# Moving the left-hand tiles of a two-layer attention kernel by 32 bytes, loading its first keys in three groups, and splitting its first weights earlier

## The chip, the cores and the metric

The kernel runs on one core of one Trainium2 chip. The metric is the device time of one execution in microseconds, lower is better; the time of a kernel is the median of several executions. The engines are named as in the profile: PE (TensorE, matmul), PEld (TensorE's weight load), DVE (VectorE), ACT (ScalarE), POOL (GpSimd) and SP (SyncE, which here issues most DMAs). SBUF is the on-chip memory with 128 partitions, PSUM the memory that matmuls write.

## What is computed

Two layers, each an attention block followed by a block in which only 8 chosen tokens go through a feed-forward net. Everything is float32, with 2048 tokens of width 1024 and 32 heads of width 32:

```python
def _A_ref(x, wqkv, wo):
    qkv = (x @ wqkv).reshape(B, S, 3, H, Dh).transpose(2, 0, 3, 1, 4)
    q, k, v = qkv[0], qkv[1], qkv[2]
    p = softmax(einsum("bhqd,bhkd->bhqk", q, k) * Dh ** -0.5)
    o = einsum("bhqk,bhkd->bhqd", p, v)
    return o.transpose(0, 2, 1, 3).reshape(B, S, D) @ wo

def _B_ref(x, w_r, w_gate, w_up, w_down):
    r = x @ w_r
    idx = argsort(-r)[:, :8]
    ...
    y = (silu(x_sel @ w_gate) * (x_sel @ w_up)) @ w_down
    return x + scatter(y * sigmoid(r_sel))

x = A_x
x = x + _A_ref(_layernorm(x), A_wqkv, A_wo)
x = x + _B_ref(_layernorm(x), B_w_r, B_w_gate, B_w_up, B_w_down)
x = x + _A_ref(_layernorm(x), A_wqkv, A_wo)
x = x + _B_ref(_layernorm(x), B_w_r, B_w_gate, B_w_up, B_w_down)
```

## The kernel before

`layer(n, ...)` is called for n = 0 and n = 1; its order of instructions is written out by hand. Each call has three stages.

**Projection** (`L559` to `L770`). Tokens go in four chunks (c = 0 to 3) of 512. A tile of 128 tokens is loaded (`ln_load`), its statistics are made on DVE and POOL (`ln_stat`, `L137` and `L138` on POOL), it is normalised in place (`ln_norm`, `L599`), transposed on PE (`ln_tr`, `L612`) and kept as a high part `xh` (ACT, `L613`) and a remainder `xl` (DVE, `L617`). The weight matrix comes in twelve blocks `wb` of 1 MB for each chunk: `load_w` issues the DMA into one of two `wraw` tiles, `split_w` makes a high part `wh` (ACT, `L584`) and a remainder `wl` (POOL, `L585`). Blocks 0 to 3 give queries, 4 to 7 keys, 8 to 11 values. A product of two float32 matrices is three passes, wh·xh, wl·xh and wh·xl (`passes`, `L634`), with 128x128 stationary operands and 512 moving columns. A block is two steps of 24 matmuls, so 48 matmuls. For queries and keys the weights are stationary and `xh`, `xl` move; for values it is the other way about. Step k counts from 0 to 95; b = k % 24 and c = k // 24. Before the first step of a block, `split_w` of the next block and `load_w` of the one after it are put in the program. Queries and keys go through tiles `hi` and `lo` to DRAM (`qh`, `ql`, `kh`, `kl`), values through `vn` to `vd`.

The first keys that attention needs (head group 0) are loaded back from DRAM into `ks0` by `load_k`: 12 DMAs for the 1536 tokens of chunks 0 to 2 after step (2, 23), 12 more for the last 512 tokens after step (3, 3), as `KEYS_AT` says. After step (2, 20) come two DMAs of ones and the 12 DMAs of the first two query tiles (`load_q`). All these are issued by SP, in program order, with the weight loads and the stores; an instruction of SP that waits holds up all behind it. In the fourth chunk PE also makes the first maxima of the scores (`pre_group`, `L523`).

**Attention** (`L772` to `L908`). 32 units of 16 steps. A step has four matmuls for a later unit's row maxima (`L523`), eight for the scores (`L538`), the exponentials on ACT into a tile `P` (`L878`) and eight for P·v (`L804`). A unit ends with the copy of its output to SBUF (`o<-pv`, `L829`). A head group is four units; even groups read keys from `ks0`, odd groups from `ks1`. POOL adds up the `P` tiles (`L814`).

**Output** (`L913` to `L1032`). o·wo in three passes again (`L991`), residual, the second layer norm, the choice of 8 tokens and the feed-forward, whose steps for layer 0 are spread into the projection of layer 1.

**Where the tiles lie.** A tile has the same byte address in all partitions. Pools are stacks: most grow from the left end of SBUF, those with side "right" from the right end. All left-hand tiles come after the small constants of pool `cons`, so a constant's size moves all of them. In the program as built, left-hand data tiles start at multiples of 64 bytes (layer 0's `xh` at 47424, layer 1's `wh` at 51520), right-hand ones at 32 past a multiple of 64 (layer 0's `wh` at 163808). Layer 0 has `wraw`, `wh`, `wl` and `xt` on the right, `xh`, `xl`, the query tiles and the outputs on the left. Layer 1 has `wraw`, `wh`, `wl`, `xt`, `xh` and `xl` all on the left and the query tiles on the right. In both layers `ks0` and the feed-forward's first weights are on the right, `ks1`, `P`, `v`, `acc` and the operands of `L991` on the left.

At the start of layer 0 the order is: loads of three token tiles and of weight blocks 8 and 9, statistics and normalisation of tokens tiles 0 and 1, `ln_tr(0)`, `ln_tr(1)`, then `split_w(2)` of block 8 in two halves, then the first step.

Of the kernel before, what the change touches and what calls it, by code (L numbers as in the profile page):

```python
# [8 lines left out]
F32 = mybir.dt.float32  # L9
# [9 lines left out]
S, D, H, DH, F = 2048, 1024, 32, 32, 3584  # L19
# [20 lines left out]
SLOT_ROWS = (64, 33)  # L40
SUM_AT = 22

KEYS_AT = {(2, 23): slice(0, 3 * 512), (3, 3): slice(3 * 512, S)}


def unit_events(last):
# [11 lines left out]
def tile_kernel(ctx, tc, x, wqkv, wo, w_r, w_gate, w_up, w_down, out):  # L58
# [8 lines left out]
    cons = ctx.enter_context(tc.tile_pool(name="cons", bufs=1))  # L67
# [4 lines left out]
    def dma(out, in_):  # L72
        f = [a.bitcast(F32) if a.dtype == F32R else a for a in (out, in_)]
        sync.dma_start(f[0], f[1])

    def ps_st():
        return psum.tile([128, 512], F32, name="st", bufs=3)

    def ps_pre():
        return psum.tile([128, 1024], F32, name="pre", bufs=2)  # L80
# [11 lines left out]
    pool.memset(one_c, 1.0)  # L92
    mone = cons.tile([128, 1], F32, name="mone")
    pool.memset(mone, -1.0)
    ones32 = cons.tile([128, 32], F32, name="ones32")
    pool.memset(ones32, 1.0)
    ones_row = dram.tile([1, 8192], F32R, name="ones_row")
# [372 lines left out]
    def layer(n, src, dst, prev=None):  # L470
# [22 lines left out]
        def load_k(g, h, i, sl=slice(0, S)):  # L493
            r = 64 * (h % 2) + 32 * (i % 2)
            dma(KS[g % 2][r:r + 32, h // 2, i // 2, sl], (kl if i == 1 else kh)[g, 32 * h:32 * h + 32, sl])
# [65 lines left out]
        with ExitStack() as pst:  # L561
# [16 lines left out]
            def split_w(parts=1):  # L578
                wb, raw = RAW.pop(0)
                wh, wl = (pr_.tile([128, 2048], F32R, name=i) for i in ("wh", "wl"))  # L580
                W[wb] = [w.rearrange("p (a c) -> p a c", a=KD if wb < 8 else 4) for w in (wh, wl)]
                for i in range(parts):
                    sl = slice(2048 // parts * i, 2048 // parts * (i + 1))
                    act.copy(wh[:, sl], raw[:, sl])  # L584
                    pool.tensor_tensor(wl[:, sl], raw[:, sl], wh[:, sl].bitcast(F32), op=OP.subtract)  # L585
                    yield

            def ln_load(t):
                XT[t] = pr_.tile([128, D], F32, name="xt", bufs=3)
                dma(XT[t], src[t * 128:(t + 1) * 128, :])  # L590
# [3 lines left out]
            def ln_stat(t):  # L594
                LS[t] = ln_stats(XT[t])
# [5 lines left out]
            def ln_tr(t, wide=True):  # L601
                c, i = divmod(t, 4)
                if i == 0:
                    XC[c] = (pw.tile([128, KD, 512], F32R, name="xh"), pw.tile([128, KD, 512], F32R, name="xl"))
                xh, xl = XC[c]
                sl = slice(i * 128, (i + 1) * 128)
                ps = [(slice(0, KD), ps_pre())] if wide else [(slice(4 * j, 4 * j + 4), ps_st()) for j in range(2)]
                ps = [(asl, p.rearrange("p (a c) -> p a c", c=128)) for asl, p in ps]
                for asl, p in ps:
                    for j in range(asl.stop - asl.start):  # L610
                        a = asl.start + j
                        pe.transpose(p[:, j, :], XT[t][:, a * 128:(a + 1) * 128], ident)  # L612
                    act.copy(xh[:, asl, sl], p)  # L613

                def low():
                    for asl, p in ps:
                        dve.tensor_tensor(xl[:, asl, sl], p, xh[:, asl, sl].bitcast(F32), op=OP.subtract)  # L617
                return low
# [85 lines left out]
            if n:  # L704
                for _ in range(4):
                    prev.tick()
            lo = ln_tr(0)
            ln_load(3)
            ln_stat(2)
            lo()  # L710
            lo = ln_tr(1)
            ln_load(4)
            if not n:
                list(split_w(2))
            lo()
            ln_norm(2)
            ln_stat(3)
# [7 lines left out]
            for k, (c, wb, i) in enumerate(steps):  # L725
# [31 lines left out]
                if norm and at % 4 == 2:  # L757
                    ln_tr(t)()
                    if t + 3 < NT - n:
                        ln_load(t + 3)  # L760
                if (c, b) in KEYS_AT:
                    for j in range(3):
                        for h in range(4):
                            load_k(0, h, j, KEYS_AT[c, b])
                if (c, b) == (2, 20):
# [267 lines left out]

    x3 = dram.tile([S, D], F32, name="x3")
    layer(1, x3, out, layer(0, x, x3)).finish()


# [24 lines left out]
```

## Time and profile before

| what | value |
|---|---|
| three executions | 4647.03, 4654.71, 4658.94 us; median 4654.71 us |
| the profiled execution's own time | 4656.52 us |
| its span, first to last instruction | 4654.5 us |
| mean granted TensorE clock | 0.987 |
| projection, layer 0 / layer 1 | about 15 to 595 us / 2287 to 2900 us |
| attention, layer 0 / layer 1 | about 595 to 2049 us / 2900 to 4357 us |

The profile is of one execution. Its page gives the busy time of each engine, the span in 40 slices, the DMA queues, the chain of work that ended last, and groups of instructions with their busy time, mean length and idle time before them. The timeline lists instructions in order of time: start, length, engine, line, operation, output and inputs (for a matmul the moving operand first, then the stationary one), and in brackets how long the engine sat idle before it and what ended that. Two matmuls overlap in these records, since the end of each is modelled; the distance between their starts is what a matmul costs.

### The profile page before, as it was taken

Reading aid. Unit: us, or ns where it says so; the run is one execution under the profiler, and the core shown is the slowest. Engines: PE = TensorE matmul, PEld = TensorE weight load, DVE = VectorE, ACT = ScalarE, POOL = GpSimd, SP = SyncE. Lnnn points to the kernel's source line nnn. Section 1 sums busy time; section 2 is a strip of 40 time slices with the busy share of each in tenths; the row PEclk is TensorE's granted clock in tenths of the full one; section 3 lists DMA queues with packets and bytes.
Section 4 is the critical chain, followed back from the end, with each engine's and each line's share of the span. In section 5 each row is a group of like instructions: output and inputs, shape, how many; then the busy total and the mean of one; then the engine's idle time right before and its main releaser. Section 6 shows DMA issues by size and latency. Waiting matters only on the chain. (4 is left out here: it accounts for less than half of the span.)

```text
span 4654.5 us, 73388 instructions
## 1 busy us (share of the span) xinstructions
PE 4542.4 (98%) x29228; PEld 2697.7 (58%) x29228; DVE 3185.8 (68%) x4899; ACT 2428.1 (52%) x2562; POOL 3212.2 (69%) x1233
## 2 busy tenths in 40 slices
PE   8999999999999999999899999999999999999996
PEld 7887755545555555548577777555555555554572
DVE  2211578888888888876522215888888888887763
ACT  3222266767667676760122222776767667677400
POOL 4444378989889898944433442888889889898441
PEclk9999999999999999999899999999999999999997
DMA  5756476867777777749578674777767768676598
GB/s 184 201 179 196 141 165 145 180 149 161 170 153 168 156 168 158 181 118 262 180 247 288 218 208 128 162 168 155 172 148 171 160 150 180 147 168 159 149 257 309
DMA packets 326598, 833.26 MB, mean 179 GB/s; under 512 B 43008, under 2 KB 158720, under 8 KB 277088
## 3 DMA queue, kind: packets, MB, share of 16 engines
q1 hardware_dynamic: 272720, 476.91, 34.5%
q0 software_dynamic: 45024, 325.41, 34.5%
q10 hardware_dynamic: 8512, 26.26, 2.1%
q8 instruction: 229, 3.75, 0.3%
q14 instruction: 113, 0.93, 0.1%
HBM read 384.14 MB, written 119.24 MB: 108 GB/s over the span
## 5 line engine op out<-in xcount | busy, mean ns | idle before, releaser
L531 DVE TENSOR_REDUCE nm<-st 128x1 f32<-128x512 f32 x3916 | 2433.8, 684 | 373.4 <-PE st L523 367.4
L878 ACT ACTIVATE P<-pre 128x1024 f32<-128x1024 f32 x2048 | 1985.8, 1022 | 719.7 <-PE pre L538 521.9
L814 POOL TENSOR_TENSOR acc<-acc,P 128x2048 f32<-128x2048 f32 x434 | 2105.5, 4851 | 87.3 <-DMA P<-P 80.3
L538 PE MATMUL pre<-q,ks 64*128 64x512 f32 (+1 forms) x8192 | 1138.3, 395 | 4.2 <-ACT P L878 4.2
L804 PE MATMUL pv<-P,v 128*32 128x512 f32 x8192 | 1091.4, 605 | 4.5 <-DMA v<-vd 4.5
L523 PEld LDWEIGHTS st<-ks,q 64*128 64x128 f32 x3916 | 546.8, 184 | 907.5 <-DVE nm L531 764.2
L523 PE MATMUL st<-ks,q 64*128 64x512 f32 x3916 | 986.5, 471 | 0.4
L585 POOL TENSOR_TENSOR wl<-wraw,wh 128x2048 fp32r<-128x2048 f32 (+1 forms) x97 | 442.7, 4564 | 653.6 <-ACT wh L584 645.1
L538 PEld LDWEIGHTS pre<-q,ks 64*128 64x128 f32 (+1 forms) x8192 | 772.8, 187 | 186.6 <-ACT P L878 57.3
L817 POOL DMA_DIRECT2D P<-P x310 | 298.4, 963 | 257.5 <-PE st L523 185.0
L649 DVE TENSOR_TENSOR lo<-st,hi 128x512 fp32r<-128x512 f32 x128 | 88.5, 692 | 566.1 <-ACT hi L648 547.6
L634 PE MATMUL st<-xh,wh 128*128 128x512 f32 x1024 | 410.0, 400 | 0.0
L634 PE MATMUL st<-xh,wl 128*128 128x512 f32 x1024 | 402.0, 393 | 4.4 <-POOL wl L585 4.4
L634 PE MATMUL st<-xl,wh 128*128 128x512 f32 x1024 | 403.1, 394 | 0.0
L648 ACT CAST hi<-st 128x512 fp32r<-128x512 f32 x128 | 75.1, 586 | 538.7 <-PE st L634 533.6
L804 PEld LDWEIGHTS pv<-P,v 128*32 128x32 f32 x8192 | 162.3, 108 | 260.7 <-issue 252.5
L814 POOL TENSOR_TENSOR acc<-P 128x2048 f32<-128x2048 f32 x62 | 295.2, 4762 | 9.7 <-ACT P L878 5.2
L991 PE MATMUL pre<-woh,ohl 128*128 128x512 f32 x1024 | 245.5, 398 | 18.8 <-DVE pre L1019 13.2
L584 ACT CAST wh<-wraw 128x2048 fp32r<-128x2048 f32 (+1 forms) x97 | 183.2, 1891 | 148.2 <-PE pre L634 71.2
L991 PEld LDWEIGHTS pre<-woh,ohl 128*128 128x128 f32 x1024 | 195.3, 192 | 66.8 <-issue 17.2
L634 PEld LDWEIGHTS st<-xh,wh 128*128 128x128 f32 x1024 | 193.1, 189 | 56.4 <-issue 8.9
L634 PEld LDWEIGHTS st<-xh,wl 128*128 128x128 f32 x1024 | 193.3, 189 | 46.5 <-POOL wl L585 5.2
(249 smaller groups left out, 2961.7 us busy)
## 6 DMA issues: line engine op xcount, KB each, us to landing
P<-P POOLq DMA_DIRECT2D x310, 1024.0 KB, 8.9
wraw<-in_A_wqkv_dram SPq DMA_DIRECT2D x96, 1024.0 KB
q<-qh SPq DMA_DIRECT2D x256, 128.0 KB
ks<-kh SPq DMA_DIRECT2D x112, 256.0 KB
vd<-vn SPq DMA_DIRECT2D x32, 512.0 KB
qh<-hi SPq DMA_DIRECT2D x64, 256.0 KB
ql<-lo SPq DMA_DIRECT2D x64, 256.0 KB
kh<-hi SPq DMA_DIRECT2D x64, 256.0 KB
```

The costliest lines, as they stand in the source:

```text
L523: pe.matmul(ps[b], Q[u][rows, i, 0, qt * 128:(qt + 1) * 128], KS[(u // QC) % 2][rows, i, 0, j * 512:(j + 1) * 512], start=True, stop=True, ...
L531: dve.tensor_reduce(NM[u][:, j, 2 * i + b:2 * i + b + 1, qt], ps[b], axis=AX.X, op=OP.max, negate=True)
L538: pe.matmul(p[:, b * 512:(b + 1) * 512], KS[(u // QC) % 2][rows, i, slot, kt * 128:(kt + 1) * 128], Q[u][rows, i, slot, :], start=(slot == ...
L584: act.copy(wh[:, sl], raw[:, sl])
L585: pool.tensor_tensor(wl[:, sl], raw[:, sl], wh[:, sl].bitcast(F32), op=OP.subtract)
L634: pe.matmul(p, *pair(a, l, r), start=(a == 0 and k == 0), stop=(a == KD - 1 and k == 2))
L649: dve.tensor_tensor(lo, p, hi.bitcast(F32), op=OP.subtract)
L804: pe.matmul(PV[u][32 * h:32 * h + 32, :], V[g][:, kt, 32 * h:32 * h + 32], P[s][:, h, :], start=(kt == 0), stop=(kt == NT - 1), tile_posit ...
L814: (dve if on_dve else pool).tensor_tensor(o, a, P[u * NT + k].rearrange("p h c -> p (h c)"), op=OP.add)
L817: pool.dma_start(P[u * NT + a], P[u * NT + b], accum_op=OP.add)
L878: act.activation(P[s][:, 2 * i:2 * i + 2, :].rearrange("p h c -> p (h c)"), p, AF.Exp, scale=SCALE)
L991: pe.matmul(p[:, bl], l[:, a, :], r[a][:, bl], start=(k == 0 and a == 0), stop=(k == 2 and a == KD - 1))
```

## The change

Three edits. The keys of head group 0 for the first three chunks are loaded in three groups of 12 DMAs of 512 tokens each, after steps (2, 14), (2, 17) and (2, 20), in place of one group of 12 DMAs of 1536 tokens after step (2, 23). A constant tile of 32 bytes, which nothing reads or writes, is added to `cons`; each left-hand tile from `ones32` on moves by 32 bytes, right-hand tiles stay. And in layer 0 the first half of the split of the first weight block is put ahead of the first transposes, the second half right behind them, in place of both halves behind the second transposes.

```diff
-KEYS_AT = {(2, 23): slice(0, 3 * 512), (3, 3): slice(3 * 512, S)}
+KEYS_AT = {(2, 14 + 3 * i): slice(i * 512, i * 512 + 512) for i in range(3)}
+KEYS_AT[3, 3] = slice(3 * 512, S)
...
     pool.memset(mone, -1.0)
+    cons.tile([128, 8], F32, name="pad")
     ones32 = cons.tile([128, 32], F32, name="ones32")
...
+            first_w = split_w(2) if not n else iter(())
+            next(first_w, None)
             lo = ln_tr(0)
+            list(first_w)
             ln_load(3)
             ln_stat(2)
             lo()
             lo = ln_tr(1)
             ln_load(4)
-            if not n:
-                list(split_w(2))
             lo()
             ln_norm(2)
             ln_stat(3)
```

On the engines this moves: on ACT the two half copies `wh` (`L584`) from behind both `xh` copies to before the first and between the two; on POOL the two half subtractions `wl` (`L585`) ahead of the statistics of token tile 2; on SP the key loads as said. PE's and DVE's order stays the same.

## The prediction

> **What bounds the kernel now.** I read the page's totals first, then PE's groups, then what PE waited for.
>
> ```profile
> span 4654.5 us, 73388 instructions
> PE 4542.4 (98%) x29228; PEld 2697.7 (58%) x29228; DVE 3185.8 (68%) x4899; ACT 2428.1 (52%) x2562; POOL 3212.2 (69%) x1233
> ```
>
> ```profile
> L804 PE MATMUL pv<-P,v 128*32 128x512 f32 x8192 | 1091.4, 605 | 4.5 <-DMA v<-vd 4.5
> L634 PE MATMUL st<-xh,wh 128*128 128x512 f32 x1024 | 410.0, 400 | 0.0
> L991 PE MATMUL pre<-woh,ohl 128*128 128x512 f32 x1024 | 245.5, 398 | 18.8 <-DVE pre L1019 13.2 <-ACT ohl L944 4.7 <-DVE ohl L945 0.6
> ```
>
> ```profile
> PE st L634 <- POOL wl L585: 4.4, 2, 2.4
> ```
>
> PE is busy for 98% of the span: 4654.5 − 4542.4 leaves 112 us without it. So two things can move the time: a wait of PE that goes or comes, and the pace of the matmuls themselves. All waits of projection matmuls (`L634`) for `wl` inside the run sum to 4.4 us in two places. The pace is the larger matter, and it is not the same in the two layers. These are the first matmuls of consecutive blocks in layer 0 and layer 1, two blocks of queries or keys and two of values, each with 48 matmuls in between and no wait:
>
> ```profile
> 402.61 0.39 PE L634 MATMUL pre<-wh,xh 128*128 128x512 f32 x1
> ...
> 413.85 0.40 PE L634 MATMUL pre<-wh,xh 128*128 128x512 f32 x1
> ...
> 436.34 0.40 PE L634 MATMUL st<-xh,wh 128*128 128x512 f32 x1
> ...
> 447.54 0.40 PE L634 MATMUL st<-xh,wh 128*128 128x512 f32 x1
> ```
>
> ```profile
> 2711.59 0.39 PE L634 MATMUL pre<-wh,xh 128*128 128x512 f32 x1
> ...
> 2722.47 0.39 PE L634 MATMUL pre<-wh,xh 128*128 128x512 f32 x1
> ...
> 2744.23 0.39 PE L634 MATMUL st<-xh,wh 128*128 128x512 f32 x1
> ...
> 2755.11 0.39 PE L634 MATMUL st<-xh,wh 128*128 128x512 f32 x1
> ```
>
> A block of values takes 413.85 − 402.61 = 11.24 us in layer 0 and 2722.47 − 2711.59 = 10.88 us in layer 1; a block of queries 447.54 − 436.34 = 11.20 against 2755.11 − 2744.23 = 10.88. That is 0.234 and 0.233 us from start to start against 0.227, the same instructions on the same shapes, with nothing idle. What differs is where the operands lie. In layer 0 one operand (`xh`, `xl`) starts at a multiple of 64 bytes and the other (`wh`, `wl`) 32 bytes past one; in layer 1 both start at multiples of 64.
>
> **The 32 bytes.** After the change layer 0's `xh` lies at 47456 and its `wh` still at 163808: both are 32 past a multiple of 64, so the two operands stand in step again, as in layer 1, though both off 64. No row has two 128-row operands of this kind both at 32. The bounds: if only the step between the operands counts, layer 0 gains 0.36 us in 16 value blocks and 0.32 us in 32 query and key blocks, 5.8 + 10.2 = 16.0 us, and layer 1 keeps its pace. If the offset of 32 itself costs, layer 0 gains nothing and layer 1 loses as much as layer 0 could have gained. Attention has all four combinations, and so says which is nearer. These are the output copies that end a group of four units: even groups (`ks0`, right) and odd ones (`ks1`, left), first layer 0 with queries on the left, then layer 1 with queries on the right.
>
> ```profile
> 964.24 0.59 ACT L829 COPY o<-pv 128x512 f32<-128x512 f32 x1
> ...
> 1147.36 0.59 ACT L829 COPY o<-pv 128x512 f32<-128x512 f32 x1
> ...
> 1330.51 0.59 ACT L829 COPY o<-pv 128x512 f32<-128x512 f32 x1
> ...
> 3269.46 0.59 ACT L829 COPY o<-pv 128x512 f32<-128x512 f32 x1
> ...
> 3452.70 0.59 ACT L829 COPY o<-pv 128x512 f32<-128x512 f32 x1
> ...
> 3635.88 0.59 ACT L829 COPY o<-pv 128x512 f32<-128x512 f32 x1
> ```
>
> Layer 0: even 183.12 us (queries at 0, keys at 32), odd 183.15 (both at 0). Layer 1: even 183.24 (both at 32), odd 183.18 (queries 32, keys 0). The attention matmuls with two operands at 32 pay 0.09 us in 183, 0.05%, against those with both at 0; an offset that cost 3% by itself would show here as several us. But the mixed groups aren't slower either, so these 64-row pairs hide the effect that the 128-row matmuls show, and the evidence is one-sided. I take the first bound, slightly cut: one block starts at the slow clock, and the fourth chunk has other matmuls between. 15.5 us off.
>
> For the rest of attention the same rows give the price: `q`, `ks` all at 32 is the 183.24 case, 0.1 us a group, under 1 us in all. `P` and `v` (`L804`) are both on the left and move together; I take zero, with 1 to 3 us either way for the range. `L991` has both operands on the left and keeps its step: zero. The other engines read and write the moved tiles too. They are off the path: in layer 0's attention PE is busy for 1448.32 of 1454 us, whatever they do.
>
> ```profile
> 595.00:2049.00 1454.00, 1448.32 (x10850) 723.37 (x10846) 1257.73 (x2021) 1022.75 (x1084) 1274.90 (x403) 1.00 0.73 160
> ```
>
> The Trainium skill's page "SBUF — State Buffer", section "Who interferes with whom", speaks against this term: it gives TensorE two independent read ports, one for the moving operand and one for the weight load, and says that PE never waits on anyone. By that rule the place of one operand beside the other can't matter and this term is 0; the 3% between the layers is then left without a cause, and no run here has yet shown that it is the place. It is the third case below.
>
> **The keys.** PE's two waits for `wl` come from SP's queue. The rows of layer 0, by SP, ACT and PE, and the block's start and the next one's; then the same block of layer 1:
>
> ```profile
> 438.10 2.39 SPq L74 DMA_DIRECT2D ks<-kh  x4
> ...
> 445.36 0.39 SPq L74 DMA_DIRECT2D wraw<-in_A_wqkv_dram  x1
> ```
>
> ```profile
> 454.47 1.90 ACT L584 CAST wh<-wraw 128x2048 fp32r<-128x2048 f32 x1 [6.14 <-DMA wraw<-in_A_wqkv_dram]
> ```
>
> ```profile
> 458.74 0.40 PE L634 MATMUL st<-xh,wh 128*128 128x512 f32 x1
> 461.08 0.50 PE L634 MATMUL st<-xh,wl 128*128 128x512 f32 x1 [1.94 <-POOL wl L585]
> ...
> 473.70 0.39 PE L634 MATMUL st<-xh,wh 128*128 128x512 f32 x1
> ```
>
> ```profile
> 2765.99 0.39 PE L634 MATMUL st<-xh,wh 128*128 128x512 f32 x1
> ...
> 2781.19 0.39 PE L634 MATMUL st<-xh,wh 128*128 128x512 f32 x1
> ```
>
> The twelve key DMAs hold SP from 438.10 to 445.36 (7.26 us), their data goes ahead of the weights', and ACT gets the block 6.14 us late. The block then takes 473.70 − 458.74 = 14.96 us against 11.20, 3.76 more: the wait and the slower matmuls behind it. In layer 1 it is 2781.19 − 2765.99 = 15.20 against 10.88, 4.32 more. With the keys gone from there the weight load is issued some 7 us earlier, more than the lateness: 8.1 us off.
>
> The keys come back as 36 DMAs, at about 7.26 / 12 = 0.6 us each, in three places. Behind the first two groups wait one pair of key stores and the two weight loads of this row:
>
> ```profile
> 392.44 7.04 SPq L74 DMA_DIRECT2D wraw<-in_A_wqkv_dram  x2
> ```
>
> They are for the blocks that start at 413.85 and, 11.24 us on, at 425.1. The first has 21.4 us, of which `wh` and `wl` (1.9 and 4.6 us, rows below) take 6.5; some 7 us of SP's time still leaves 7 for the transfer. I put these two groups at nothing, covered by that lead; without it they would cost what a late block costs, some 4 us. The third group stands ahead of the ones, the query loads and this weight load:
>
> ```profile
> 425.20 0.39 SPq L74 DMA_DIRECT2D wraw<-in_A_wqkv_dram  x1
> ```
>
> ```profile
> 437.54 1.91 ACT L584 CAST wh<-wraw 128x2048 fp32r<-128x2048 f32 x1
> ```
>
> ```profile
> 439.54 4.62 POOL L585 TENSOR_TENSOR wl<-wraw,wh 128x2048 fp32r<-128x2048 f32 x1 [7.59 <-ACT wh L584]
> ```
>
> Issued 7.3 us later, at 432.5, it would have to land by 437.5 to cost nothing. `wl` now ends at 439.54 + 4.62 = 444.16; PE needs it for the second matmul of the block at 447.54, so 3.6 us of lateness are free. The bounds are 0 (the load had several us to spare, as ACT shows no wait for it) and the whole of 3.76 and 4.32 us again. A third of the old group (a third of the bytes) is in front, so I take 0.5 us in each layer: 1 us back, 7.1 off.
>
> **The first weights.**
>
> ```profile
> 11.92 1.29 DVE L133 BATCH_NORM_STATS2 bst<-xt 128x6 f32<-128x512 f32 x2 [0.56 <-DMA xt<-in_A_x_dram]
> ...
> 14.51 3.79 ACT L584 CAST wh<-wraw 128x1024 fp32r<-128x1024 f32 x3
> ...
> 18.05 0.80 PE L634 MATMUL pre<-wl,xh 128*128 128x512 f32 x1 [1.64 <-POOL wl L585]
> ...
> 21.51 4.61 POOL L585 TENSOR_TENSOR wl<-wraw,wh 128x2048 fp32r<-128x2048 f32 x1
> 21.58 5.09 DVE L599 TENSOR_SCALAR xt<-xt,mv,rs 128x1024 f32<-128x1024 f32 x1 [1.60 <-POOL rs L138]
> ...
> 26.72 1.03 PE L612 MATMUL st<-ident,xt 128*128 128x128 f32 x6 [0.59 <-DVE xt L599]
> ```
>
> Token tile 2 was issued behind block 8's weights on the same queue and is there by 11.92, so the weights are too. The first half can be copied before 12 us in place of 14.51, and PE's first matmuls stop waiting for `wh` and `wl`: up to 4 us earlier. But token tile 3 holds PE next. Its normalisation (21.58, 5.09 us) ends with POOL's 4.61 us subtraction that began 0.07 us before it; its statistics now come behind both half subtractions on POOL, so it moves forward by 1 to 1.5 us only, and the 26.72 row with it. If the DMA comes late, ACT holds back the first `xh` by up to 1 us. Between −4 and +1 I take −1.3, by that row.
>
> **The sum.** −15.5 − 7.1 − 1.3 = −23.9 us against the profiled execution, 4656.5 us (span 4654.5 and 2.0 around it): 4632.6. That execution is 1.8 us above the median of the three, 4654.7, so for the median 4631.
>
> **The rivals.**
> - *The offset of 32 itself is slow* (slower). From the first block of layer 0 on, every 128-row three-pass matmul with an operand at 32 takes 0.0067 us more: layer 0 stays, layer 1 loses 16.0, the 1536 matmuls of `L991` lose 10.2, the waits give back 8.4: +17.8, so 4672. With a second charge for the second operand it is 16 + 16 + 10 more, about 4715. For it: each slow block has an operand at 32, no fast one has. Against it: the 183.24 us groups.
> - *The 32 bytes do nothing* and the layers differ for another reason: −8.4, so 4646. Against it: the pace is constant over all of layer 0's blocks and changes with nothing else that I can name.
> - *The wait moves one block ahead*: the third key group makes block 37 of the projection as late as block 38 was. The keys give nothing, −15.5 − 1.3 and perhaps 1 us more lost: 4639. For it: SP's order; against it: the 3.6 us of slack.
>
> **How the numbers follow.** Forecast 0.64, offset slow 0.17, nothing from the 32 bytes 0.12, wait moved 0.07. A measurement of this kernel can't tell less than 0.3%, 14 us, from no change: faster means under 4641, slower over 4669. The forecast's own range is 4620 to 4641 (start and keys at their better bounds and attention's 3 us at the low end, no more than half the keys at the high end). Faster: 0.62 of it and half of the moved wait, 0.66. Same: the rest of these and the 0.12, 0.17. Slower: 0.17. The overall range leaves out the slow rival alone: 4616 to 4656, with some us for the spread of 4647 to 4659 shown by three runs.
>
> **What would show it.** Layer 0's blocks at 10.88 us with a matmul every 0.227 us, layer 1's unchanged, attention groups within 183.1 to 183.3: the 32 bytes as forecast. Layer 1's blocks at 11.2 us or `L991` slower: the first rival. No wait of `L634` for `wl` near the fourth chunk's third block: the keys; one at its second block: the moved wait. First `L634` matmul before 14 us with token tile 3's transposes near 25.4: the start. I am wrong if layer 0's pace stays at 0.233.

## The result and the profile after

The changed kernel takes 4643.6 us (median of 15 executions, 4639.5 to 4649.0) against 4652.9 us before (median of 15, 4647.0 to 4663.3) in the same comparison: a ratio of 0.9977 with a 95% interval of 0.9969 to 0.9984. That is 9 us, where some 24 were forecast. The profiled execution took 4647.36 us, with a span of 4645.5.

The page of the changed kernel opens with the span and the busy time of each engine. The projection's lines have moved down by two: its matmuls are now `L636`, the transposes `L614`, the split `L586` and `L587`, the normalisation `L601`. The output's have moved by three: its product is `L994`.

```profile
span 4645.5 us, 73445 instructions
PE 4535.0 (98%) x29228; PEld 2692.4 (58%) x29228; DVE 3181.2 (68%) x4899; ACT 2428.6 (52%) x2562; POOL 3211.9 (69%) x1233
```

PE is busy 7.4 us less (4542.4 before) with the same 29228 matmuls. The timeline of PE has the first matmuls of the same blocks of 48 as those shown of before: in layer 0 two blocks of values and four of queries and keys, then in layer 1 two and three.

```profile
399.24 0.40 PE L636 MATMUL pre<-wh,xh 128*128 128x512 f32 x1
...
410.44 0.40 PE L636 MATMUL pre<-wh,xh 128*128 128x512 f32 x1
...
432.83 0.40 PE L636 MATMUL st<-xh,wh 128*128 128x512 f32 x1
...
444.03 0.40 PE L636 MATMUL st<-xh,wh 128*128 128x512 f32 x1
...
455.23 0.40 PE L636 MATMUL st<-xh,wh 128*128 128x512 f32 x1
...
466.43 0.40 PE L636 MATMUL st<-xh,wh 128*128 128x512 f32 x1
...
2707.02 0.39 PE L636 MATMUL pre<-wh,xh 128*128 128x512 f32 x1
...
2717.90 0.39 PE L636 MATMUL pre<-wh,xh 128*128 128x512 f32 x1
...
2750.54 0.39 PE L636 MATMUL st<-xh,wh 128*128 128x512 f32 x1
...
2762.29 0.39 PE L636 MATMUL st<-xh,wh 128*128 128x512 f32 x1
...
2773.17 0.39 PE L636 MATMUL st<-xh,wh 128*128 128x512 f32 x1
```

- *Pace.* A block of values in layer 0 takes 410.44 − 399.24 = 11.20 us (11.24 before), a block of queries 444.03 − 432.83 = 11.20 (11.20 before). Layer 1 stays at 2717.90 − 2707.02 = 10.88. So layer 0's pace hardly moved, and layer 1, which now has both operands 32 past a multiple of 64, did not move at all.
- *Late blocks.* In layer 0 the block that waited takes 466.43 − 455.23 = 11.20 us instead of 14.96, in layer 1 2773.17 − 2762.29 = 10.88 instead of 15.20. The block ahead of it is new on the list in layer 1: 2762.29 − 2750.54 = 11.75, 0.87 more than its neighbours.

The list of PE's waits shows the late blocks, the start and the output product:

```profile
PE pre L994 <- DVE pre L1022: 15.2, 8, 5.4
...
PE st L614 <- DVE xt L601: 8.8, 3, 5.1
...
PE st L636 <- POOL wl L587: 0.6, 1, 0.6
```

The two waits of query and key blocks for `wl`, 4.4 us, are one of 0.6 now. The waits of the transposes for normalised tokens grew from 5.7 (two) to 8.8 (three): some 5.1 us of each sum is one wait in layer 1 that stayed, and in layer 0 the wait for token tile 3 grew from 0.59 to 3.49. `L994`, the output product, waits 15.2 us for DVE against 13.2, and all its waits grew from 18.8 to 21.6, though the change only moves its tiles, all by the same 32 bytes.

### The profile page after: what moved, and what is told of

It reads as the page before. It is cut to its first block, busy times and chain, and to the rows that moved or that the text cites. A ratio compares the mean times of both kernels' runs of the same rounds, so it can differ in the third digit from the quotient of the medians.

```text
span 4645.5 us, 73445 instructions
## 1 busy us (share of the span) xinstructions
PE 4535.0 (98%) x29228; PEld 2692.4 (58%) x29228; DVE 3181.2 (68%) x4899; ACT 2428.6 (52%) x2562; POOL 3211.9 (69%) x1233
## 5 line engine op out<-in xcount | busy, mean ns | idle before, releaser
L587 POOL TENSOR_TENSOR wl<-wraw,wh 128x2048 fp32r<-128x2048 f32 (+1 forms) x97 | 442.4, 4561 | 643.5 <-ACT wh L586 634.8
L636 PE MATMUL st<-xh,wh 128*128 128x512 f32 x1024 | 406.4, 397 | 0.0
L636 PE MATMUL st<-xh,wl 128*128 128x512 f32 x1024 | 401.4, 392 | 0.6 <-POOL wl L587 0.6
L636 PE MATMUL st<-xl,wh 128*128 128x512 f32 x1024 | 401.7, 392 | 0.0
L994 PE MATMUL pre<-woh,ohl 128*128 128x512 f32 x1024 | 247.6, 400 | 21.6 <-DVE pre L1022 15.2
L586 ACT CAST wh<-wraw 128x2048 fp32r<-128x2048 f32 (+1 forms) x97 | 183.7, 1894 | 145.9 <-PE pre L636 78.5
L994 PEld LDWEIGHTS pre<-woh,ohl 128*128 128x128 f32 x1024 | 196.9, 194 | 70.4 <-issue 19.9
L636 PEld LDWEIGHTS st<-xh,wh 128*128 128x128 f32 x1024 | 192.5, 188 | 56.4 <-issue 9.0
L636 PEld LDWEIGHTS st<-xl,wh 128*128 128x128 f32 x1024 | 192.4, 188 | 43.1
```

What stands on the lines that cost most here:

```text
L636: pe.matmul(p, *pair(a, l, r), start=(a == 0 and k == 0), stop=(a == KD - 1 and k == 2))
L994: pe.matmul(p[:, bl], l[:, a, :], r[a][:, bl], start=(k == 0 and a == 0), stop=(k == 2 and a == KD - 1))
```

## The experiments

The question after the result: why do layer 0's matmuls start every 233 ns and layer 1's every 227, if not by the offset modulo 64? Two theories, and a third that blames nothing in particular. *Step theory*: what counts is the distance between `xh` and `wh` modulo some larger power of two. *Side theory*: what counts is that one operand lies at the left end of SBUF and the other at the right. *Third theory*: something else of layer 0.

**Padding further, and moving the weights.** All three start from the changed kernel. The first two only change the size of the pad (40 numbers are 160 bytes; 168 in its place are 672), the third only the side of layer 0's weight pool.

```diff
-    cons.tile([128, 8], F32, name="pad")
+    cons.tile([128, 40], F32, name="pad")
```

```diff
-            pr_ = pst.enter_context(sbuf(f"pw{n}", bufs=2, side=None if prev else "right"))
+            pr_ = pst.enter_context(sbuf(f"pw{n}", bufs=2, side=None))
```

> The changed kernel with a pad of 160 bytes in place of 32: layer 0's xh at 47584, wh at 163808, a distance that is a multiple of 512 (but 512 past a multiple of 1024); after the change as given it was 128 past a multiple of 256. Step theory (the pace depends on the distance of the two operands modulo a power of two, 64 was too small): with 512 as the modulus, layer 0's blocks fall from 10.92 us first matmul to last to 10.65, as in layer 1, 48 x 0.27 = 13 us off, so about 4631 us. Side theory (what counts is that one operand lies at the left end of SBUF and the other at the right): blocks stay at 10.9 to 11.0 us and the time at 4642 to 4646. Third theory (something else of layer 0, not the place): the same as the side theory here.

> The changed kernel with a pad of 672 bytes: layer 0's xh at 48096, wh at 163808, a distance that is a multiple of 1024 (and not of 4096). Step theory with 512 or 1024 as the modulus: blocks of layer 0 at 10.65 us, about 4631 us; if the 160-byte pad stays slow and this one is fast, the modulus is 1024. Side theory and third theory: 10.9 to 11.0 us, 4642 to 4646.

> The changed kernel with layer 0's pool of wraw, xt, wh and wl on the left, where xh and xl lie (wh 76128, xh 108896; distance a multiple of 4096). Side theory: blocks of layer 0 at 10.65 us as in layer 1, 48 x 0.27 = 13 us off, 4629 to 4632. Step theory: the same, since the operands also come in step; the two are told apart by the padded kernels. Third theory (something else of layer 0): blocks stay at 10.9 us, 4642 to 4646.

In one comparison with the kernel before (4668.0 us): 160 bytes 4643.5 us, ratio 0.9957 (0.9940 to 0.9973); 672 bytes 4642.3, 0.9956 (0.9939 to 0.9972); weights on the left 4641.9, 0.9945 (0.9929 to 0.9962). The timeline of the 160-byte pad has layer 0's blocks of values, then of queries:

```profile
391.93 0.39 PE L636 MATMUL pre<-wh,xh 128*128 128x512 f32 x1
...
402.81 0.39 PE L636 MATMUL pre<-wh,xh 128*128 128x512 f32 x1
...
424.57 0.39 PE L636 MATMUL st<-xh,wh 128*128 128x512 f32 x1
...
435.45 0.39 PE L636 MATMUL st<-xh,wh 128*128 128x512 f32 x1
```

402.81 − 391.93 = 10.88 us, 435.45 − 424.57 = 10.88: layer 1's pace, in layer 0, with the operands still at opposite ends. The other two kernels have the same 10.88. So the side theory and the third theory fall, and the modulus is at most 512.

**Which modulus, and can layer 1 be made slow?** Two more pad sizes (104 numbers, 416 bytes, and 32 numbers, 128 bytes), and the weights on the left again with a gap of 128 bytes between the two pools in both layers:

```diff
-    cons.tile([128, 8], F32, name="pad")
+    cons.tile([128, 104], F32, name="pad")
```

```diff
+            pst.enter_context(sbuf(f"gap{n}")).tile([128, 32], F32, name="gap")
             pw = pst.enter_context(sbuf(f"pj{n}", bufs=2))
```

> The changed kernel with a pad of 416 bytes: the distance of layer 0's xh and wh is 256 past a multiple of 512. If the modulus is 256: blocks of layer 0 at 10.65 us as with 160. If it is 512: 10.9 us or more.

> The changed kernel with a pad of 128 bytes: the distance is 32 past a multiple of 512, where it was 160 past before the change (a matmul every 233.5 ns), 128 after it (232.4) and 0 with the pad of 160 (226.7). Step theory with any distance off the modulus slow: 232 to 234 ns, blocks at 10.9 to 11.0. If the cost grows with the distance: about 227 to 229 ns, 10.65 to 10.75.

> Layer 0's weights on the left beside xh as in the same-side run, but with a gap tile of 128 bytes between the two pools in both layers, so that the distance of xh from wh is 128 past a multiple of 512 in layer 0 and in layer 1 too. Step theory with 512 (or 256) as the modulus: blocks of both layers at 10.9 us first to last, a matmul every 232 ns, although all operands lie on one side; layer 1, which was at 10.65 in every run so far, becomes slow for the first time. Side theory: 10.65 us in both layers.

One execution each, beside 4666.5 us for the kernel before: 416 bytes 4637.4 us, 128 bytes 4663.2, the gap 4676.3; being single executions, they are read by their pace. Their totals hold more than that: from the last `o<-pv` copy of layer 0 to layer 1's first projection matmul the 128-byte pad took 284.7 us and the gap 283.3, against 272 to 279 in the other twelve profiles, and why stays open. Blocks of values with 416 bytes, blocks of queries with 128 bytes, and blocks of queries in layer 1 of the kernel with the gap:

```profile
392.15 0.39 PE L636 MATMUL pre<-wh,xh 128*128 128x512 f32 x1
...
403.03 0.39 PE L636 MATMUL pre<-wh,xh 128*128 128x512 f32 x1
```

```profile
436.75 0.40 PE L636 MATMUL st<-xh,wh 128*128 128x512 f32 x1
...
447.95 0.40 PE L636 MATMUL st<-xh,wh 128*128 128x512 f32 x1
```

```profile
2759.49 0.40 PE L636 MATMUL st<-xh,wh 128*128 128x512 f32 x1
...
2770.68 0.40 PE L636 MATMUL st<-xh,wh 128*128 128x512 f32 x1
```

10.88 us at a distance of 256, 11.20 at 32, and layer 1 is slow for the first time: 2770.68 − 2759.49 = 11.19, though all its operands lie at one end. Together, with the distance of `wh` from `xh` in the programs as built, and the spacing of matmuls (for each block the median distance of three starts, divided by three; mean over a layer's 48 blocks):

| kernel | layer 0: distance mod 256 | layer 0: ns | layer 1: distance mod 256 | layer 1: ns |
|---|---|---|---|---|
| before, keys alone | 160 | 233.7 | 0 | 227.0 to 227.1 |
| after, pad alone, late first weights | 128 | 232.6 to 232.8 | 0 | 227.0 to 227.1 |
| pad 128 | 32 | 233.3 | 0 | 226.7 |
| pad 160, 672, 416 | 0 | 227.0 | 0 | 226.9 to 227.0 |
| weights on the left | 0 | 226.9 | 0 | 227.1 |
| weights on the left, gap 128 | 128 | 233.4 | 128 | 233.0 |

Of the powers of two the modulus is 256: 128 is slow, and 256 past a multiple of 512 is fast. The place of the pair as a whole doesn't matter: in step, both operands lay 64, 96, 192 or 224 past a multiple of 256, and all of these ran at 227 ns. The cost is one of in step or out of it: 32 bytes off costs as much as 128 or 160, some 6 ns per matmul. Over 48 x 48 matmuls of a layer, 2304 x (232.8 − 227.0) ns = 13.4 us stayed unclaimed in the changed kernel. The three timed kernels in step lie 0.0020 to 0.0032 below the changed kernel's ratio of 0.9977, which is 9 to 15 us, each by an interval of some 8 us either way.

**Which pair must be in step?** The 160-byte pad with `wh` alone moved off by 128, in both layers:

```diff
-                wh, wl = (pr_.tile([128, 2048], F32R, name=i) for i in ("wh", "wl"))
+                wh = pr_.tile([128, 2048], F32R, name="wh")
+                if not W:
+                    pr_.tile([128, 32], F32, name="gap", bufs=1)
+                wl = pr_.tile([128, 2048], F32R, name="wl")
```

> The pad of 160 bytes, and a gap of 128 bytes between wh and wl, in both layers: now xh, xl and wl are in step modulo 256 and wh alone is 128 off them. In a block of queries or keys the matmuls go wh.xh, wl.xh, wh.xl with w stationary. If what counts is the weight load that runs beside a matmul (the next one's) against the data that this matmul streams: the intervals that begin with wl.xh and wh.xl are slow (next load wh), those that begin with wh.xh fast (next load wl). If what counts is a matmul's own two operands: those of wh.xh and wh.xl are slow, of wl.xh fast. In both cases two of three are slow, the mean is 230 to 231 ns, and blocks take 10.8 us in both layers.

A block of values, then one of queries, in layer 0:

```profile
401.23 0.39 PE L639 MATMUL pre<-wh,xh 128*128 128x512 f32 x1
...
412.22 0.39 PE L639 MATMUL pre<-wh,xh 128*128 128x512 f32 x1
...
434.19 0.39 PE L639 MATMUL st<-xh,wh 128*128 128x512 f32 x1
...
445.39 0.40 PE L639 MATMUL st<-xh,wh 128*128 128x512 f32 x1
```

The one execution took 4660.7 us, beside 4657.9 for the kernel before. Neither prediction came out. Queries and keys, with the weights stationary, are as slow as with everything out of step (445.39 − 434.19 = 11.20 us; intervals that begin with wh·xh, wl·xh, wh·xl of 233, 235 and 232 ns in the median of layer 0), so no interval is fast. Values, with the weights moving, lose a third of it (412.22 − 401.23 = 10.99; 233, 226 and 228 ns). Which reads meet, and why, stays open; the rule that holds over the other kernels is that all four tiles be in step.

**Each edit alone.** The keys in three groups alone, the pad of 32 bytes alone, and the change without the early first weights:

```diff
-KEYS_AT = {(2, 23): slice(0, 3 * 512), (3, 3): slice(3 * 512, S)}
+KEYS_AT = {(2, 14 + 3 * i): slice(i * 512, i * 512 + 512) for i in range(3)}
+KEYS_AT[3, 3] = slice(3 * 512, S)
```

> The kernel before with the keys in three groups as the only edit. My step by step account: the late block of layer 0 (14.73 us first to last) falls to 11.0 and that of layer 1 (14.97) to 10.65, less 0.9 us at the block after it in layer 1, as seen in the changed kernel: 7.2 us off, 4645 to 4646 (ratio 0.9985). Rival (the keys give nothing, since another block becomes late): 4652 to 4654, ratio 1.000.

```diff
     pool.memset(mone, -1.0)
+    cons.tile([128, 8], F32, name="pad")
```

> The kernel before with the pad of 32 bytes as the only edit. Modulus 256: the distance goes from 160 to 128 past a multiple of 256, still out of step; blocks of layer 0 fall from 11.0 us to 10.92, 48 times 0.05 to 0.08 us, so 2.5 to 4 us off; late blocks and start as before. Ratio 0.999 to 1.000, about 4 of the 9 us of the whole change at most. My forecast had given this edit 15.5 us: ratio 0.9967.

```diff
-            first_w = split_w(2) if not n else iter(())
-            next(first_w, None)
             lo = ln_tr(0)
-            list(first_w)
...
             ln_load(4)
+            if not n:
+                list(split_w(2))
```

> The changed kernel with the first weights split late, as before. In the changed kernel block 9 starts at 31.7 us instead of 33.4, but in the six other runs that split early it starts at 33.0 to 34.4 (best apart), because PE waits longer for token tile 3 and then runs at the slow clock. If early weights are worth nothing on the whole: block 9 at 33.2 to 33.6 here, and the time within 2 us of the changed kernel, ratio 0.998 of before. If they are worth the 1.3 us that I forecast, the same within what can be timed: the block's start decides, 33.3 against the mean of the early ones, 33.2.

Keys alone: ratio 0.9978 (0.9969 to 0.9988), in the comparison in which before was 4668.0 us, so 6 to 14 us off. Pad alone: 0.9990 (0.9980 to 0.9999); without early weights: 0.9974 (0.9965 to 0.9984), both beside a before of 4657.9 us. The once late blocks of the two layers with the keys alone:

```profile
458.67 0.40 PE L635 MATMUL st<-xh,wh 128*128 128x512 f32 x1
...
469.87 0.40 PE L635 MATMUL st<-xh,wh 128*128 128x512 f32 x1
...
2770.05 0.39 PE L635 MATMUL st<-xh,wh 128*128 128x512 f32 x1
...
2780.93 0.39 PE L635 MATMUL st<-xh,wh 128*128 128x512 f32 x1
```

11.20 and 10.88 us: nothing late is left, 3.76 + 4.32 = 8.1 us off. The block ahead of it is late in some runs and not in others: over the twelve kernels that carry the keys' edit, the changed kernel among them, it takes up to 0.6 us too long in layer 0 and up to 1.6 in layer 1.

The pad alone gives the pace of the changed kernel (232.7 ns) and no more. Its interval is 0.5 to 9 us off, and the pace accounts for 2304 x 1.0 ns = 2.3. The old late blocks are still there, that of layer 1 with 17.8 us in this profile, and its span of 4655.7 us is no shorter than before.

The early weights can't be told from nothing in the time. Block 9, the second block that layer 0 runs, starts at 33.4, 33.3, 33.0 and 32.6 us in the four kernels so far that split late (before, keys alone, pad alone, this one; mean 33.1) and at 31.7, 33.0, 34.2, 34.3, 34.0, 33.2, 34.4 and 34.1 in the eight that split early (mean 33.6). What takes the gain away stands in the start of the changed kernel and of the 672-byte pad. The changed kernel's timeline, and its windows (columns: stretch, length, then the busy time of PE, PEld, DVE, ACT and POOL, granted clock, DMA share, GB/s):

```profile
13.88 0.50 PE L636 MATMUL pre<-wh,xh 128*128 128x512 f32 x1 [0.76 <-DVE xl L619]
...
16.73 0.81 DVE L601 TENSOR_SCALAR xt<-xt,mv,rs 128x1024 f32<-128x1024 f32 x1 [1.11 <-POOL rs L140]
...
19.85 4.54 POOL L587 TENSOR_TENSOR wl<-wraw,wh 128x2048 fp32r<-128x2048 f32 x1
19.92 5.01 DVE L601 TENSOR_SCALAR xt<-xt,mv,rs 128x1024 f32<-128x1024 f32 x1 [0.94 <-POOL rs L140]
...
24.99 1.26 PE L614 MATMUL st<-ident,xt 128*128 128x128 f32 x8 [3.49 <-DVE xt L601]
```

```profile
25.00:28.00 3.00, 3.00 (x17) 2.46 (x18) 2.83 (x5) 1.18 (x2) 0.00 (x0) 1.00 0.22 72
```

The same in the kernel with the 672-byte pad:

```profile
25.20 1.97 PE L614 MATMUL st<-ident,xt 128*128 128x128 f32 x8 [3.52 <-DVE xt L601]
```

```profile
25.00:28.00 3.00, 2.80 (x11) 2.61 (x12) 2.21 (x5) 1.17 (x2) 0.00 (x0) 0.50 0.00 0
```

PE starts earlier, runs out of work earlier, and waits longer for token tile 3: 3.5 us in both. In one run it comes back at the full clock, in the other at 0.50, with transposes of 1.97 us in place of 1.26. Block 9 then starts at 34.2 in place of 31.7. Of the eight kernels that split early, the changed kernel's profile is the only one with the full clock from 25 to 28 us; the other seven have 0.50 there, five of them behind a pause of about 3.5 us, two (the 160- and the 416-byte pad) behind one of 2.64 and 2.74. The Trainium skill's page "TensorE: Matmul & The Clock Gate", section "Part 1: The HAM clock gate", has the clock decided over free-running windows of some 3.4 us. By that rule a pause of about that length would cool PE in one run and not in another, as in the two rows above; the pauses of 2.64 and 2.74 us are shorter than such a window, and it doesn't explain them by itself.

**A version faster than both.** The 160-byte pad, and the split of block 9 in four pieces, so that POOL's subtraction doesn't hold DVE for 4.5 us; with the first weights early, and with them late:

```diff
-                    list(split_w())
+                    list(split_w(1 if n or k else 4))
```

> The 160-byte pad, and block 9's split (copies wh and subtractions wl, at the first step of layer 0) in four parts instead of one. In all runs DVE's normalisation of token tile 3 takes 5.0 us beside POOL's 4.5 us subtraction and 0.8 us without it. If it only waits for POOL's instruction to end: it gets in after the first of four parts, 1.2 us, ends near 22 instead of 25, and the first block ends some 3 us earlier, near 30 us; the total is some 3 us below the 160-byte pad, 4627 to 4641 on its chip, ratio to before 0.995. If DVE is held back by POOL's work as such, whatever the size of the pieces: normalisation stays near 5 us, no gain over the 160-byte pad.

> The best version so far (160-byte pad, block 9's split in four parts) with the first weights split late as in the kernel before. If early weights help once token tile 3 no longer holds PE up: block 9 starts 1 to 1.5 us later than the 29.2 us with them, and the total is 1 us more. If they help nothing: 29.2 and the same total, ratio 0.9948.

With early weights: 4640.9 us, ratio 0.9948 (0.9934 to 0.9962), beside 4666.5 before. With late ones: 4630.2 us, 0.9940 (0.9926 to 0.9953), beside 4657.9 on another chip. The two intervals overlap; both lie clear of the change as given (0.9969 to 0.9984), though each was compared with the kernel before and never with the changed kernel directly. They also overlap that of the 160-byte pad alone (0.9940 to 0.9973), so what the four pieces add isn't shown in the time, only at the start. The start with early weights:

```profile
20.55 5.49 POOL L587 TENSOR_TENSOR wl<-wraw,wh 128x512 fp32r<-128x512 f32 x4
...
20.62 1.77 DVE L601 TENSOR_SCALAR xt<-xt,mv,rs 128x1024 f32<-128x1024 f32 x1 [0.94 <-POOL rs L140]
...
22.88 1.04 PE L614 MATMUL st<-ident,xt 128*128 128x128 f32 x8
...
29.24 0.39 PE L636 MATMUL pre<-wh,xh 128*128 128x512 f32 x1
```

DVE gets in behind the first piece: 1.77 us in place of 5.01, and the transposes wait for nothing. Block 9 starts at 29.2 us with early weights and at 32.3 with late ones, so in this version, by one profile of each, the early weights are worth 3 us at the start, more than the 1 to 1.5 expected. The total doesn't show it; the span from the last projection matmul of layer 1 to the end alone ranged from 1751 to 1761 us over the fourteen profiles.

## Why the prediction was right or wrong

- **What bounds the kernel** held: the time moved with PE's pace and PE's waits. The block behind the late one of layer 0 starts at 466.43 in place of 473.70, 7.3 us earlier: 1.7 from the start, 3.8 from the late block, and 38 of 48 blocks of the pace below, 1.7, make 7.2.
- **The 32 bytes: the failed step.** The step was "I take the first bound, slightly cut", that is, that "the two operands stand in step again" when both are 32 past a multiple of 64: 15.5 us. Both paces were read rightly, and that the place of one operand against the other makes the difference is now shown. But the step is modulo 256, not 64. The change took the distance from 160 to 128, out of step to out of step, and the pace from 233.7 to 232.8 ns: about 2304 x 0.9 ns = 2.1 us. The only two distances that the profile of before had were 160 and 0, so it could not tell a modulus of 64 from one of 256; with the addresses 47424 and 163808 at hand, the other powers of two that fit should have been bounds of their own.
- **The keys** came out as the sum said: 3.76 and 4.32 us off, 0 and 0.87 back (0.5 in each was taken), −7.2 against −7.1. The first two groups cost nothing, as put.
- **The first weights** gave −1.7 us in the profiled run (PE's first matmul 15.61 to 13.88, the transposes of tile 3 26.72 to 24.99, forecast near 25.4), −1.3 were forecast. That it came out near the forecast is luck: in the other seven early-split profiles PE came out of its pause at half the clock, and block 9 started at 33.0 to 34.4 us, against a mean of 33.1 with late splits. What was missed is that a pause of PE behind an earlier start can cost the clock.
- **The sum.** Measured in the two profiles: −2.1 − 7.2 − 1.7 = −11.0 us; the spans differ by 9.0. The 2 us between lie behind the projection: from the last `o<-pv` copy of layer 0 to layer 1's first projection matmul it took 275.7 us against 272.7, 3.0 more, and behind layer 1's last copy 1.5 less. No edit was shown to cause this; the first stretch ranged from 272 to 285 us over the fourteen profiles. The fifteen executions of each kernel told these 9 us from no change, so the 14 us that the prediction gave as the least it could tell was too coarse.
- **The rivals.** *The offset of 32 itself is slow* is refuted: layer 1 with both operands at 32 stays at 10.88 us. *The 32 bytes do nothing* gave 4646 and stands nearest to the 4643.6 measured; but its reason, that the layers differ by something else, is refuted by the pads. What the Trainium skill's page "SBUF — State Buffer", section "Who interferes with whom", says of TensorE's two independent read ports, and that PE never waits on anyone, would make the place of the tiles worth nothing; 233 against 227 ns by the distance alone differs from it, and the measurement decides. *The wait moves one block ahead* happened in part, by up to 1.6 us, not by 3.8.

## What to carry to other kernels

When two stages run the same matmuls on the same shapes at two steady paces, compare the byte addresses of the moving and the stationary tiles: here, in step modulo 256 bytes was worth 2.5 to 3% of the pace, and a pad of 160 bytes bought it. Two measured distances don't give a modulus: list every power of two that fits them before pricing a shift. And an engine that is fed earlier only waits longer if the next input is not earlier too; first look for what holds that up.

## What the runs showed of the hardware

- 128-row matmuls with 512 moving columns and a weight load for each start every 227 ns when the tiles of both operands are a multiple of 256 bytes apart, and every 232 to 234 ns at distances of 32, 128 or 160 past one, whether they lie at one end of SBUF or at both (at one end only 0 and 128 were tried). The output product's matmuls, of the same shape and with their tiles in step in every kernel, also start every 227 ns. Attention's 64-row matmuls don't show it: queries and keys lay at 0, 32, 128 and 160, and a group of four units took 183.0 to 183.3 us in every profile. Its 32-column matmuls were not tried out of step: `P` and `v` lie in step in every kernel.
- With only one of four tiles out of step the cost depends on its role: the full 0.32 us a block when it is stationary, 0.11 when it moves.
- A DVE normalisation of 0.8 us takes 5.0 beside a POOL subtraction of 4.5 us and 1.8 beside the same subtraction in four pieces.
- A pause of PE of about 3.5 us ended at the full clock in one run and at half of it in five; one of 2.64 us and one of 2.74 also ended at half.
